# Running sums of logs and angles as two fp32r products each, at new places in the instruction stream

## The chip, the cores and the metric

One core of a Trainium2 chip (trn2) runs the whole kernel. The time is device microseconds of one execution, the median of several. All runs told here were in the fast state of the chip (one core, mean granted TensorE clock 0.957 to 0.992 over the span). Every timed version was run in rounds beside the kernel before on the same chip.

## The reference

A linear-attention block with complex decays (4 batches, 8 heads, 768 steps, 48 columns a head) followed by a two-layer block with the activation h·cos(h). Cut to what matters:

```python
def _attn_ref(q, k, v, a_re, a_im):
    mag = np.sqrt(a_re * a_re + a_im * a_im)
    scale = np.minimum(mag, 0.999) / (mag + 1e-06)
    a_re_n, a_im_n = (a_re * scale, a_im * scale)
    for t in range(S):                       # state is multiplied by a complex number each step
        new_re = ar * S_re - ai * S_im       # ar, ai: a_re_n, a_im_n of step t
        new_im = ar * S_im + ai * S_re
        S_re, S_im = (new_re + kv, new_im)   # kv: outer product of k[t] and v[t]
        y[:, :, t] = einsum(q[:, :, t], S_re)

def _moe_ref(x, w_in, w_out):                # x: (3072, 384)
    h = x @ w_in                             # w_in: (384, 2048)
    return (h * np.cos(h)) @ w_out
```

A chain of complex multiplications is a running sum of logarithms of the magnitudes and a running sum of the angles. The kernel takes both as products with a triangle of ones on TensorE. These are the two products that the change rewrites.

## The kernel before

The 3072 rows are 24 chunks of 128 steps; two chunks are a group, so there are 12 groups. The kernel is a software pipeline: while TensorE does the two layers of group n, the logs, angles and trigonometry of group n + 1 are made ready. `weave` merges lists of work by a fraction of the stage: a pair like `0.22, 0.24` says where in the stage a list is laid. All of TensorE's instructions are chained in that order; VectorE and ScalarE get an order from the scheduler.

```python
    def log_steps(g, i, n):          # "..." marks cuts
        chain(nc.scalar.activation(out=m2, in_=re, func=AF.Square))
        chain(nc.scalar.activation(out=sq, in_=im, func=AF.Square))
        vector.tensor_tensor(out=m2, in0=m2, in1=sq, op=ALU.add)
        yield
        special(out=m2, in_=m2, func=AF.Ln, bias=tiny_b)
        ...
        special(out=rs, in_=rs, func=AF.Ln, scale=EPS, bias=one_b)
        special(out=sq, in_=mag, func=AF.Ln)
        special(out=sq, in_=sq, func=AF.Exp, scale=-1.0)
        yield
        vector.tensor_tensor(out=m2, in0=m2, in1=rs, op=ALU.subtract)    # the logs, tile lg
        yield
        vector.tensor_tensor(out=mag, in0=mag, in1=sq, op=ALU.mult)      # three steps that only
        ...                                                              # the angles need

    def p_powers(g, i):              # running sum of logs (lgs), then powers P = exp, Q = exp(-)
        ...
        matmul(ps, lhsT=sums[g >= PEG], rhs=cut(x["lg"], i, 1), start=True, stop=True)
        special(out=cut(x["P"], i, 1), in_=ps, func=AF.Exp)
        special(out=cut(x["Q"], i, 1), in_=ps, func=AF.Exp, scale=-1.0)

    def g_phase(g, i):               # running sum of angles (phs); i: which chunk of the group
        if i:
            g_carry(g, i)            # chunk 1 needs the last phase of chunk 0
        matmul(ps, lhsT=turns[g >= PEG], rhs=cut(x["tan"], i, 1), start=True, stop=not early)
        ...
        scalar.copy(out=ph.bitcast(I32), in_=ps)                          # whole turns
        vector.tensor_tensor(out=ph, in0=ps, in1=ph.bitcast(I32), op=ALU.subtract)

    def prods(g):
        for i in range(G):
            yield lambda i=i: p_powers(g, i)
        yield lambda: g_angle(g, 0, G)                                    # arctangent
        yield lambda: g_carry(g, 0)
        yield lambda: (p_even(g, 0, G), p_apply(g, 0, G))                 # corrects P and Q, applies them

    def seventh(g, p, part):         # second layer as seven products; 0, 3, 5, 6 share one sum
        summed = p in (0, 3, 5, 6) and not alone
        ps = x["sum"] if summed else x["op"]
        ...                          # 16 matmuls of 192 columns; the sum goes on without a restart
        if p in (1, 3, 4, 5) or alone:   # VectorE reads the partial sum after product 3
            added = vector.scalar_tensor_tensor(out=part_, in0=..., scalar=scale, in1=part_, ...)

    for n in range(2, NG):
        weave(..., (logs(n + 1), 0.0, 0.02), ...,
              (prods(n + 1), 0.22, 0.24), ..., (products(n - 1, 3, 7), 0.4, 0.56),
              (phases(n + 1), 0.4, 0.56), (keys(n + 1), 0.53, 0.66), ...)
```

One thing in it matters later. The products 0, 3, 5 and 6 of the second layer pile up in one accumulator, and its state after product 3 is itself a result. So product 5 cannot start before VectorE has read the partial sum.

## Time and profile before

| | kernel before |
|---|---|
| time, median (lowest to highest) | 684.94 us (684.42 to 685.08, 3 runs) |
| span of the profiled run | 681.9 us |
| TensorE busy | 653.7 us, 96% |
| VectorE busy | 480.3 us, 70% |
| ScalarE busy | 382.5 us, 56% |

The busy times are shares of the whole span. TensorE has no room, and the other two have room on average. The average says nothing about where in a group they are full, which is what this case turns on. The lines themselves are in the prediction.

### The profile page before, as it was taken

The page shows a single profiled execution, that of the slowest core. Times are in us where ns is not written, and L with a number is a line of the kernel's source. Part 1 is how long each engine was busy: PE and PEld are TensorE (multiplying, and loading weights), DVE is VectorE, ACT ScalarE, POOL GpSimd, SP SyncE. Part 2 cuts the span into 40 slices and gives each one's busy share as a digit, 9 for nine tenths or more (in the row PEclk, how much of TensorE's full clock was granted, in tenths as well). Part 3 has the DMA queues.
Part 4 walks back from the last instruction along what each step waited for, and adds up shares of the span by engine and source line. Part 5 has one row for each costly group of instructions (what it writes and reads, how often), then busy time and mean ns, then how long its engine had stood idle before and what let it go on. Part 6 is the DMA issues. An engine that isn't in the chain of part 4 may idle for free.

```text
span 681.9 us, 10685 instructions
## 1 busy us (share of the span) xinstructions
PE 653.7 (96%) x4060; PEld 577.7 (85%) x4060; DVE 480.3 (70%) x782; ACT 382.5 (56%) x710; POOL 27.3 (4%) x45
## 2 busy tenths in 40 slices
PE   5788999999999999999999999999999999999996
PEld 5686676886899889899899889999899889999895
DVE  4889988468867877777777777767777768762251
ACT  5769784473474475466476476366466467332330
POOL 2012000000000000000000000000000000000000
PEclk8979999999999999999999999999999999999998
DMA  9777717706537557656657657565766653264000
GB/s 245 177 232 230 187 59 159 201 1 143 160 70 140 153 126 164 170 131 154 184 127 158 180 128 161 158 145 122 205 139 130 196 128 83 104 141 127 24 6 24
DMA packets 232954, 94.97 MB, mean 139 GB/s; under 512 B 208814, under 2 KB 221361, under 8 KB 232892
## 3 DMA queue, kind: packets, MB, share of 16 engines
q1 hardware_dynamic: 226396, 68.68, 44.6%
q0 software_dynamic: 5632, 25.17, 11.0%
q8 instruction: 34, 0.56, 0.4%
q10 hardware_dynamic: 864, 0.33, 0.2%
q14 instruction: 28, 0.23, 0.1%
HBM read 69.35 MB, written 24.81 MB: 138 GB/s over the span
## 4 chain that ended last, share of the span: by engine, by line
PE 84%; DMA 5%; DVE 5%; ACT 4%; issue 1%; DVEq 0%; ACTq 0%
PE hp L683 31%; PE op L683 17%; PE sum L683 15%; PE sc L683 6%; PE yp L683 5%; PE sp L683 3%; PE lgs L683 2%; DMA raw<-in_moe_w_out_dram 2%; PE phs L683 2%; DMA qT<-moved 2%; DVE w_in L672 1%; ACT raw L672 1%; DVE w_out L672 1%; PE yr L683 1%; DMA im<-in_a_im_dram 1%
## 5 line engine op out<-in xcount | busy, mean ns | idle before, releaser
L683 PE MATMUL hp<-xT,w_in 128*128 128x256 f32 x1152 | 253.6, 382 | 0.6 <-ACT xT L672 0.6
L683 PEld LDWEIGHTS hp<-xT,w_in 128*128 128x128 f32 x1152 | 220.1, 191 | 32.2 <-ACT xT L672 1.0
L702 ACT ACTIVATE gate<-hp,half_pi_b 128x512 f32<-128x512 f32 x96 | 65.9, 687 | 126.6 <-PE hp L683 126.6
L672 DVE TENSOR_TENSOR gate<-hp,gate 128x512 f32<-128x512 f32 x96 | 65.6, 683 | 60.0 <-ACT junk L672 60.0
L683 PE MATMUL op<-w_out,gate 128*128 128x192 f32 (+1 forms) x448 | 101.6, 375 | 2.3 <-DVE w_out L672 2.3
L683 PEld LDWEIGHTS op<-w_out,gate 128*128 128x128 f32 x448 | 75.8, 190 | 22.5 <-DVE w_out L672 3.5
L672 ACT ACTIVATE junk<-hp 128x512 bf16<-128x512 f32 x96 | 56.6, 590 | 0.0
L683 PE MATMUL sum<-t_s,s 128*128 128x192 f32 x320 | 55.3, 326 | 0.0
L683 PEld LDWEIGHTS sum<-t_s,s 128*128 128x128 f32 x320 | 52.6, 190 | 0.0
L683 PEld LDWEIGHTS sc<-qT,kT 96*128 96x128 f32 x384 | 47.5, 192 | 5.3 <-issue 2.8
L683 PE MATMUL sc<-qT,kT 96*128 96x128 f32 x384 | 49.5, 276 | 2.4 <-DMA qT<-moved 1.3
L672 DVE TENSOR_TENSOR atm<-sc,causal 128x512 f32<-128x512 f32 x48 | 32.8, 686 | 21.3 <-PE sc L683 21.1
L672 ACT ACTIVATE ot<-sum 128x192 f32<-128x192 f32 x30 | 9.5, 321 | 59.8 <-PE sum L683 59.8
L672 DVE SCALAR_TENSOR_TENSOR ot<-op,ot 128x192 f32<-128x192 f32 x31 | 11.0, 355 | 41.2 <-ACT ot L672 26.1
L698 ACT ACT_TABLE_LOAD x26 | 33.4, 1283 | 4.0 <-DMA ident<-ident_const 3.6
L683 PE MATMUL yp<-atm,v 128*48 128x128 f32 x352 | 33.5, 277 | 0.0
L683 PEld LDWEIGHTS sp<-v,ks 128*96 128x96 f32 x320 | 29.7, 165 | 1.8 <-issue 1.0
L683 PE MATMUL sp<-v,ks 128*96 128x48 f32 x320 | 29.6, 245 | 0.0
L683 PE MATMUL sum<-w_out,gate 128*128 128x192 f32 x160 | 29.6, 329 | 0.0
L683 PE MATMUL yp<-qT,state 96*48 96x128 f32 x304 | 29.6, 272 | 0.0
L683 PE MATMUL op<-t_a,gate 128*128 128x192 f32 x160 | 29.0, 332 | 0.0
L672 ACT CAST tan<-phs 128x384 int32<-128x384 f32 x24 | 11.5, 479 | 30.8 <-PE phs L683 30.6
(123 smaller groups left out, 949.2 us busy)
## 6 DMA issues: line engine op xcount, KB each, us to landing
moved<-tr SPq DMA_DIRECT2D x20, 768.0 KB
raw<-in_moe_w_in_dram POOLq DMA_DIRECT2D x16, 768.0 KB, 5.7
raw<-in_moe_w_out_dram POOLq DMA_DIRECT2D x16, 768.0 KB, 4.9
kT<-moved SPq DMA_DIRECT2D x40, 192.0 KB
qT<-moved SPq DMA_DIRECT2D x10, 768.0 KB
k<-in_k_dram SPq DMA_DIRECT2D x24, 192.0 KB
q<-in_q_dram SPq DMA_DIRECT2D x24, 192.0 KB
v<-in_v_dram SPq DMA_DIRECT2D x24, 192.0 KB
```

Of the source, the lines that this page charges most:

```text
L672: ins = getattr(self.engine, op)(**kw)
L683: chain(nc.tensor.matmul(out, **kw), "tensor")
L698: chain(nc.scalar.preload_act_table_set(table))
L702: chain(nc.scalar.activation(func=func, **kw))
```

## The change

The intent: a full fp32 product of 384 columns costs TensorE 0.645 us from its start to the next. The type fp32r is meant to be cheaper a product; that it keeps less of a float is what the halves are for, and no run here measured it. A float is split into a high half (its copy in the new type) and a low half (the remainder), each times ones and summed in one accumulator; that this is the same number at half the price was the author's assumption. The two passes together took 0.348 us in the changed kernel, and the runs below that keep the halves passed the comparison with the reference. The halves cost one ScalarE copy (high; 0.84 us for 768 columns, 0.52 for 384) and one VectorE instruction (low; 0.95 and 0.56). The angles of the second chunk can be split only after the carry of the first; so its first 96 rows are split early, and the last 32 once the carry is in. To give the halves time, the products are moved: logs from 0.22–0.24 to 0.27–0.31 of the stage, the angles from 0.4–0.56 to 0.475 and 0.52. Groups 0 and 1 stay as they were. The diff, cut to its core:

```diff
+    def halves(g, x, i, n, scale, part=slice(0, C)):
+        hi, lo, all_ = (cut(t, i, n)[part] for t in (X[g]["hi"], X[g]["lo"], x))
+        scalar.activation(out=hi, in_=all_, func=AF.Copy, scale=scale)
+        vector.scalar_tensor_tensor(out=lo, in0=all_, scalar=scale, in1=hi.bitcast(F32),
+                                    op0=ALU.mult, op1=ALU.subtract)
+    def g_halves(g):
+        if g >= PEG:
+            new_halves(g)
+            halves(g, X[g]["lg"], 0, G, 1.0)
+    def summed_up(ps, g, i, name, ones):
+        ...
+        for half in "hi", "lo":
+            matmul(ps, lhsT=exact, rhs=cut(X[g][half], i, 1), start=(half == "hi"),
+                   stop=(half == "lo"))
@@ p_powers
-        matmul(ps, lhsT=sums[g >= PEG], rhs=cut(x["lg"], i, 1), start=True, stop=True)
+        summed_up(ps, g, i, "lg", sums[0])
@@ g_carry
+        if g >= PEG:
+            at = X[g]["tan"]
+            if i == 0:
+                new_halves(g)
+                halves(g, at, 0, 1, 1.0 / math.pi)
+                halves(g, at, 1, 1, 1.0 / math.pi, slice(0, C - 32))
+            else:
+                halves(g, at, i, 1, 1.0 / math.pi, some)
@@ prods
+        yield lambda: g_halves(g)
         for i in range(G):
             yield lambda i=i: p_powers(g, i)
@@ the stages
-    weave((second(0, 1), 0.0, 0.35), (phases(2), 0.0, 0.1), (keys(2), 0.1, 0.4),
+    weave((second(0, 1), 0.0, 0.35), (phases(2), 0.2, 0.3), (keys(2), 0.3, 0.45),
-              (prods(n + 1), 0.22, 0.24), (second(n - 1, 1), 0.4, 0.56),
-              (products(n - 1, 3, 7), 0.4, 0.56), (phases(n + 1), 0.4, 0.56),
+              (prods(n + 1), 0.27, 0.31), (second(n - 1, 1), 0.4, 0.56),
+              (products(n - 1, 3, 7), 0.4, 0.56), (phases(n + 1)[:1], 0.475, 0.475), (phases(n + 1)[1:], 0.52, 0.52),
```

(Cut: the constants' pools, a scratch buffer that is `re` in place of `rs`, and the ones copied once into the new type.)

More of the change, by code (lines that the diff above doesn't have):

```diff
@@ L15 @@
 I32 = mybir.dt.int32
+F32R = mybir.dt.float32r
 BF16 = mybir.dt.bfloat16
@@ L530, in fast_path, with constant @@
     carry_np = np.where(step_np == C - 1, np.float32(math.pi), np.float32(0.0))[:, None]
-    def constant(array, name, queue=nc.scalar):
-        t = consts.tile(list(array.shape), F32, name=name)
+    def constant(array, name, queue=nc.scalar, pool=consts):
+        t = pool.tile(list(array.shape), F32, name=name)
         queue.dma_start(out=t, in_=nc.inline_tensor(array, name=name + "_const").ap())
@@ L570, in fast_path @@
             load(0, names, i)
-    ident = constant(np.eye(C, dtype=np.float32), "ident")
-    sums = [constant(sums_np[0], "sums")]
-    turns = [constant(sums_np[0] * np.float32(1.0 / math.pi), "turns")]
-    last = constant(last_np, "last")
+    ident = constant(np.eye(C, dtype=np.float32), "ident", pool=stage["pool"])
+    sums = [constant(sums_np[0], "sums", pool=stage["pool"])]
+    turns = [constant(sums_np[0] * np.float32(1.0 / math.pi), "turns", pool=stage["pool"])]
+    last = constant(last_np, "last", pool=stage["pool"])
     carry = constant(carry_np, "carry")
@@ L752, in log_steps @@
         yield
-        junk = msb.tile([C, DM], BF16, tag="below", name="below", bufs=1) if n == 1 else rs
+        junk = stage["pool"].tile([C, DM], BF16, tag="below", name="below", bufs=1) if n == 1 else re
         scalar.activation(out=junk, in_=re, func=AF.Relu, scale=-1.0,
@@ L759, in g_log, with new_halves @@
             pass
+    def halves(g, x, i, n, scale, part=slice(0, C)):
[3 more added lines that the diff above has]
+                                    op0=ALU.mult, op1=ALU.subtract)
+    def new_halves(g):
+        for name, tag in ("hi", "rs"), ("lo", "lo"):
+            X[g][name] = gt.tile([C, G * DM], F32R, tag=tag, name=name)
+    def g_halves(g):
[3 more added lines that the diff above has]
+    def summed_up(ps, g, i, name, ones):
+        if g < PEG:
+            matmul(ps, lhsT=ones, rhs=cut(X[g][name], i, 1), start=True, stop=True)
+            return
+        for half in "hi", "lo":
+            matmul(ps, lhsT=exact, rhs=cut(X[g][half], i, 1), start=(half == "hi"),
+                   stop=(half == "lo"))
     def p_powers(g, i):
@@ L824, in g_phase @@
             g_carry(g, i)
-        matmul(ps, lhsT=turns[g >= PEG], rhs=cut(x["tan"], i, 1), start=True, stop=not early)
-        if early:
+        if not early:
+            summed_up(ps, g, i, "tan", turns[0])
+        else:
+            matmul(ps, lhsT=turns[0], rhs=cut(x["tan"], i, 1), start=True, stop=False)
             matmul(ps, lhsT=last, rhs=before(n), start=False, stop=True)
@@ L1184, in fast_path @@
     load(1, ("re", "im", "k", "q"))
-    sums.append(constant(sums_np[1], "sums_turned", nc.sync))
-    turns.append(constant(sums_np[1] * np.float32(1.0 / math.pi), "turns_turned", nc.sync))
+    ones = constant(sums_np[1], "sums_turned", nc.sync, stage["pool"])
+    exact = consts.tile([C, C], F32R, name="exact")
     early = [weight(dst, src) for dst, src in into[:RAW]]
+    chain(nc.gpsimd.tensor_copy(out=exact, in_=ones), "gpsimd")
     Ordered.by_hand = True
```

## The prediction

> **What bounds the kernel now.** I read the page's busy shares first, then its forty slices, then the waits of TensorE alone, then a timeline of one group of two chunks (a group takes about 51 us in the steady part).
>
> ```profile
> PE 653.7 (96%) x4060; PEld 577.7 (85%) x4060; DVE 480.3 (70%) x782; ACT 382.5 (56%) x710; POOL 27.3 (4%) x45
> ...
> PE   5788999999999999999999999999999999999996
> ```
>
> TensorE is busy 653.7 of 681.9 us, and the 28 us of idle time lie almost wholly in the first four slices (the start, 17 us each). From slice five on the row is all nines. So in the steady part a microsecond of TensorE stream that is removed is a microsecond of the kernel, unless a wait takes its place. The waits of TensorE alone show how few there are now:
>
> ```profile
> PE phs L683 <- ACT tan L702: 4.2, 2, 2.8
> PE lgs L683 <- DVE lg L672: 2.8, 1, 2.8
> ...
> PE phs L683 <- DVE tan L672: 2.1, 4, 0.8
> PE sc L683 <- DMA qT<-moved: 1.3, 2, 0.9
> ```
>
> The first two are in the start. The third has two parts: the start, and group 2 at 108 and 113 us. The last is two groups in which the turned queries land 0.4 and 0.9 us late. The lgs and phs of groups 3 to 11 wait for nothing. What the change touches are lgs (running sum of logs) and phs (running sum of angles), one product of 384 columns each per chunk. TensorE's timeline around the ones of group 6:
>
> ```profile
> 310.89 1.45 PE L683 MATMUL lgs<-lg,sums_turned 128*128 128x384 f32 x4
> 312.28 0.43 PE L683 MATMUL yp<-atm,v 128*48 128x128 f32 x4
> ...
> 319.48 0.81 PE L683 MATMUL phs<-tan,turns_turned 128*128 128x384 f32 x2
> 320.12 2.76 PE L683 MATMUL op<-w_out,gate 128*128 128x192 f32 x16
> 322.72 2.76 PE L683 MATMUL sum<-t_s,s 128*128 128x192 f32 x16
> 325.32 0.81 PE L683 MATMUL phs<-tan,turns_turned 128*128 128x384 f32 x2
> 325.97 2.81 PE L683 MATMUL sum<-w_out,s 128*128 128x192 f32 x16
> 328.61 16.57 PE L683 MATMUL hp<-xT,w_in 128*128 128x256 f32 x76
> ```
>
> Columns: start, length, what, count. One product leaves two records (x40 records for 20 products). Starts are what counts: 320.12 - 319.48 = 0.64 us for one product, and 5.20 us of other products lie between the two phs.
>
> [...]
>
> **The change, part by part.**
>
> Groups 0 and 1 keep the old products. Groups 2 to 11 have 20 lgs and 20 phs. Removed: 40 x 0.64 = 25.6 us. Added: 80 single passes x 0.16 = 12.8 us. Gain in the stream: 12.8 us. This is the whole possible gain, but for waits of today that could vanish as well.
>
> Added elsewhere, per group: ScalarE one copy of 768 columns (0.84) and three of 384 (0.5 each), 2.3 us; VectorE one of 768 (0.95) and three of 384 (0.55 each, as the state update of 384 takes), 2.6 us. Over ten groups 23 and 26 us, to 59% and 74%. Both have room on average; in a timeline of the stretch from 299 to 318 us, though, ScalarE has hardly a gap, and there lie logs, guard and exponentials.
>
> The logs' halves are taken early, and the change puts lgs one or two products later, so I see lgs ready about 0.7 us before TensorE gets there: no wait. For the first phs I follow the instruction order of the changed kernel by hand: after lgs come four exponentials (1.2 us to the last start, 0.5 for it), table load 1.28, arctan 0.85, carry 0.62, copy 0.5, remainder 0.55, in all 5.5 us, against 6.5 us of products in between (20 of 192 columns, 0.326 each from the rows above). The second guard block, fetched about 0.75 us later because the copy delays the first on ScalarE, now sits ahead of the P and Q correction on VectorE. It makes the first phs some 0.2 us late in about four groups: 0.8 us in all.
>
> **The second phs is the term that I think costs.** It needs the carry out of the first. The steps today:
>
> ```profile
> 320.32 0.48 ACT L672 CAST tan<-phs 128x384 int32<-128x384 f32 x1 [1.67 <-PE phs L683]
> 320.83 0.56 DVE L672 TENSOR_TENSOR tan<-phs,tan 128x384 f32<-128x384 f32 x1 [0.74 <-ACT tan L672]
> 321.43 0.62 DVE L672 SCALAR_TENSOR_TENSOR tan<-tan,carry 32x384 f32<-32x384 f32 x1
> ```
>
> After the carry (322.05) the old kernel has 3.1 us in hand before 325.16, when its weights are loaded. The new one adds a copy of 32 rows on ScalarE (0.5) and a remainder on VectorE (0.55): from the start of the last half-product 0.36 to the cast, 0.51, 0.60, 0.65, 0.53, 0.55, and 0.07 to TensorE, 3.27 us. And only one of the two blocks of 2.60 us stays between the two phs, as the first was moved later. TensorE has 0.16 + 2.60 + 0.16 (the high half goes first) = 2.92 us of work. Wait: 0.35 us, [...]: 0.45. Eight groups (4 to 11): 3.6 us.
>
> Group 3: one block of 2.56 us between, but VectorE does three differences of w_out ahead of the subtraction: about 1.0 us. Group 2: in the new order its two phs stand back to back, so TensorE waits the whole chain less two half-products, 3.27 - 0.32 = 2.95 us. Today its phs are late by about 0.55 and 1.1 us (108.43 where 107.85 was possible, 112.75 where 111.65), 1.65 together, which are replaced. The rows split off the second chunk help here only in that 96 of 128 are done early; the latency of an instruction is nearly the same for 32 rows.
>
> Sum: 12.8 gained + 1.65 of old waits - 0.8 - 3.6 - 1.0 - 2.95 = 6.1 us gained. 684.94 - 6.1 = 678.8, rounded to **678.5 us**. The query transfer keeps its margin, since its start (the second phs) and its end (the first scores) are still 2.6 + 20.7 us of products apart.
>
> **Rivals.** (1) No new waits: the author's placement lets the handover fit, as the queues of VectorE and ScalarE are almost empty between the two phs (3.81 and 2.62 us busy in the 9.2 us from 319.4). Then 684.94 - 12.8 - 1.65 = 670.5, the floor, just over 2% faster. Against it: the chain's own durations exceed the block. (2) VectorE or ScalarE bind around the first phs: the guard block lands late, the correction of P and Q with it, and the halves after that. I reckon up to 1.5 us per group where the carry is queued behind all of them, in seven guarded groups 8 us or so: 685 to 687. Against it: the order puts the carry ahead of some of the work in most groups. (3) The new type runs at two cycles a column, or its weights don't hide: 80 x 0.16 = 12.8 us back, about 691 with the waits. [...] (4) The transfers of queries are late in more groups since the DMA share is 0.93 to 0.98 around phs: 1 us in each of some groups, 681 to 684.
>
> **Range and chances.** The stream gain is capped at 12.8 + 1.65, so more than 2% (under 671.2) needs rival 1 nearly entire: 0.06. Slower by over 2% (698.6) needs [...] heavy waits: 0.03. Within 2%: 0.91. The range has rival 1 with small waits below and rival 2 above: 671.8 to 686.
>
> **What would show it.** In the changed profile: lgs and phs as 40 single records each, starts 0.16 us apart in a run (0.32: rival 3); TensorE busy near 641 us; a line "PE phs <- DVE lo" or "DVE tan" in its waits with about 8 us over some 10 to 20 times, longest near 3 us at group 2; the group's period shortened by 0.7 to 0.9 us. Wrong would be: no such line and a time near 670 (rival 1); single waits over 1 us at the first phs with P and Q work just ahead on VectorE (rival 2); sc waiting on qT in more than three groups (rival 4).

## The result, and the profile after

The changed kernel took 691.99 us (690.16 to 693.81, 4 runs), beside 685.01 us (684.42 to 685.86, 4 runs) for the kernel before. The ratio is 1.0101 with a 95% interval of 1.0072 to 1.013. (Ratios here are the mean time of one kernel's fast runs over that of the other's in the same rounds, so not quite the ratio of the medians quoted.) It is 1% slower: inside the class "within 2%" that the prediction gave 0.91, but on the wrong side of zero and 6 us above the upper end of the range.

The busy shares of the changed kernel, from its page:

```profile
PE 647.9 (94%) x4060; PEld 576.7 (84%) x4060; DVE 503.5 (73%) x822; ACT 403.1 (59%) x750; POOL 27.6 (4%) x46
...
PE   6787998999999999999999999999999999999996
```

TensorE is busy 5.8 us less, VectorE 23.2 and ScalarE 20.6 us more (26 and 23 were predicted), and the span is 6.5 us longer. So the idle time of TensorE grew by 12.3 us. The row of slices does not show it, because a loss of 1 us in 51 stays a nine. The waits of TensorE alone do:

```profile
PE sum L684 <- DVE ot L673: 8.0, 7, 1.8
...
PE phs L684 <- ACT hi L673: 2.8, 2, 2.4
...
PE lgs L684 <- DVE lo L673: 1.0, 2, 0.5
```

(Total us, times, longest us.) The largest new wait is neither of the two products that were changed. It is a product of the second layer, `sum`, waiting for VectorE to write `ot`. Seven times are groups 4 to 10. The timeline of group 6 after the change, thinned to what matters:

```profile
319.59 2.76 PE L684 MATMUL sum<-t_s,s 128*128 128x192 f32 x16
320.81 0.57 DVE L673 TENSOR_SCALAR raw<-raw 128x768 uint32<-128x768 uint32 x1 [3.58 <-DMA raw<-in_moe_w_in_dram]
321.28 0.95 DVE L673 SCALAR_TENSOR_TENSOR mag<-Q,lg 128x768 f32<-128x768 f32 x1
...
324.01 1.02 DVE L673 SCALAR_TENSOR_TENSOR lo<-tan,hi 128x384 fp32r<-128x384 f32 x2
324.65 0.47 PE L684 MATMUL phs<-hi,exact 128*128 128x384 f32 x1
324.95 0.95 DVE L673 TENSOR_TENSOR Q<-k,Q 128x768 f32<-128x768 f32 x1
324.96 0.34 PE L684 MATMUL phs<-lo,exact 128*128 128x384 f32 x1
325.82 0.95 DVE L673 TENSOR_TENSOR mag<-q,lg 128x768 f32<-128x768 f32 x1
326.69 0.35 DVE L673 SCALAR_TENSOR_TENSOR ot<-sum,ot 128x192 f32<-128x192 f32 x1
327.09 2.87 PE L684 MATMUL sum<-t_s,s 128*128 128x192 f32 x16 [1.79 <-DVE ot L673]
```

Product 3, at 319.59, ends at about 322.2. Its partial sum is read only at 326.69: in front of the read VectorE runs, in the trace, a guard block that waits 3.58 us for its data, the corrections of P and Q (321.28 to 324.0), the low halves, and the two instructions that apply P and Q. The first angles' product runs in time at 324.65 and 324.96. TensorE then stands idle for 1.79 us before the next product, which goes on with the same sum. Before the change the same VectorE steps stood here:

```profile
313.41 0.96 DVE L672 SCALAR_TENSOR_TENSOR mag<-Q,lg 128x768 f32<-128x768 f32 x1 [0.92 <-ACT Q L702]
...
317.89 0.95 DVE L672 TENSOR_TENSOR mag<-q,lg 128x768 f32<-128x768 f32 x1
319.74 0.36 DVE L672 SCALAR_TENSOR_TENSOR ot<-sum,ot 128x192 f32<-128x192 f32 x1 [0.90 <-issue]
```

All of P and Q was done by 318.84, 0.6 us before product 3 ended (the first angles' product starts at 319.48), and the read ran at once. The logs' product started at 310.89 then, 8.6 us before the end of product 3; it starts at 317.45 now, 4.7 us before that end. So the move of the logs' product pushed seven VectorE instructions into the stretch in which the partial sum has to be read.

From the starts of TensorE's records, group by group, the whole account in microseconds:

| | per group | in all |
|---|---|---|
| logs' pair 1.29 to 0.70, each angles' product 0.645 to 0.348 | −1.19 | −11.9 |
| old waits gone (group 2's angles 1.8, queries 1.3) | | −3.1 |
| around the first angles' product, groups 4 to 10: low half late 1.6, next `sum` late 9.6 | +1.6 | +11.2 |
| `sum` after the second angles' product, groups 4 to 10 | +0.23 | +1.6 |
| group 2 (second product 2.5, pieces 1.0), group 3 (1.35), group 11 (1.0) | | +5.8 |
| start, between the logs' products of groups 1 and 2 | | +2.0 |

That adds up to +5.6 of the +6.5 us between the two traces. The last line need not come from the change: the kernel before without its guard blocks, a run told below, was 2.3 us longer at the end of group 1's angles than the kernel before, at the same time overall.

### The profile page after: what moved, and what is told of

It reads as the page before. It is cut to its first block, busy times and chain, and to the rows that moved or that the text cites. A ratio compares the mean times of both kernels' runs of the same rounds, so it can differ in the third digit from the quotient of the medians.

```text
span 688.4 us, 10787 instructions
## 1 busy us (share of the span) xinstructions
PE 647.9 (94%) x4060; PEld 576.7 (84%) x4060; DVE 503.5 (73%) x822; ACT 403.1 (59%) x750; POOL 27.6 (4%) x46
## 4 chain that ended last, share of the span: by engine, by line
PE 67%; DVE 11%; ACT 11%; DMA 6%; issue 3%; DVEq 0%; ACTq 0%; SPq 0%
PE hp L684 33%; PE sum L684 12%; PE op L684 9%; PE sc L684 4%; PE yp L684 4%; DMA raw<-in_moe_w_in_dram 2%; DMA raw<-in_moe_w_out_dram 2%; DVE mag L673 2%; PE sp L684 2%; ACT L699 1%; ACT lg L703 1%; DVE lg L673 1%; DVE lo L673 1%; ACT raw L673 1%; PE phs L684 1%
## 5 line engine op out<-in xcount | busy, mean ns | idle before, releaser
L673 DVE TENSOR_TENSOR gate<-hp,gate 128x512 f32<-128x512 f32 x96 | 65.6, 684 | 60.2 <-ACT junk L673 60.2
L673 ACT COPY yT<-yp 48x512 f32<-48x512 f32 x44 | 25.3, 576 | 19.8 <-PE yp L684 19.3
```

What stands on the lines that cost most here:

```text
L673: ins = getattr(self.engine, op)(**kw)
```

## The experiments

Theory D: the halves add serial steps to a path that had no slack (logs, product, exponentials, table load, arctangent, carry, halves, product, carry, halves, product, trigonometry, transposes, transfer of queries). In the stream they save 1.2 us a group, but on the path they add about 4: 0.84 + 0.95 for the logs, twice 0.5 + 0.55 for the angles. What the places decide is only where the wait shows. The rivals: (A) the moved places are the whole fault; (B) the guard blocks on VectorE are; (C) the new type or the added work costs wherever it stands.

### Undoing the places, and moving alone

`old_places`: the change with the old fractions.

```diff
-   (prods(n + 1), 0.27, 0.31) ... (phases(n + 1)[:1], 0.475, 0.475), (phases(n + 1)[1:], 0.52, 0.52)
+   (prods(n + 1), 0.22, 0.24) ... (phases(n + 1), 0.4, 0.56)          # group 2 likewise
```

> The change's halves and products, but the three shifted places in the weave (corrections and lgs, first phs, group 2) as in the kernel before. Theory A (the shifted places are what makes the first partial sum's read on VectorE late, so that TensorE waits for it before it may accumulate on): lgs come 2 to 4 us earlier, the P and Q work is done before the first phs, the waits 'sum <- DVE ot' (10.0 us on the weight loads after the change) fall under 2 us, and the time is below the kernel before, 676 to 683 us. Rival B (the added work on VectorE and ScalarE is too much at this spot wherever it is put): about as the changed kernel, 689 to 694 us.

Measured: 721.16 us (719.69 to 721.82), ratio 1.0538 (1.0515 to 1.0561). Much worse, so rival A falls as it was put (undoing the places does not bring the gain): the author had reason to move the products. The wait for `ot` is gone and this took its place, in the waits of TensorE:

```profile
PE lgs L684 <- DVE lo L673: 21.0, 10, 2.9
```

Its timeline in group 6:

```profile
326.13 0.84 ACT L673 ACTIVATE hi<-lg 128x768 fp32r<-128x768 f32 x1
...
327.04 0.47 PE L684 MATMUL lgs<-hi,exact 128*128 128x384 f32 x1
327.26 0.95 DVE L673 SCALAR_TENSOR_TENSOR tan<-mag,tan 128x768 f32<-128x768 f32 x1
...
328.39 0.94 DVE L673 SCALAR_TENSOR_TENSOR tan<-tan,im 128x768 f32<-128x768 f32 x1
329.26 0.95 DVE L673 SCALAR_TENSOR_TENSOR lo<-lg,hi 128x768 fp32r<-128x768 f32 x1
330.26 0.44 PE L684 MATMUL lgs<-lo,exact 128*128 128x384 f32 x1 [2.74 <-DVE lo L673]
```

The high half is done at 326.97, and the low half starts at 329.26, behind steps that only the angles need. This is the line that later led to the fast version. There is a second cost, the clock. The granted clock, by stretches around three of these stalls (columns: stretch, length, busy of PE, PEld, DVE, ACT, POOL, clock, DMA share, GB/s):

```profile
267.00:282.00 15.00, 12.26 (x88) 11.51 (x87) 9.91 (x14) 9.12 (x16) 0.76 (x1) 0.77 0.47 111
325.00:340.00 15.00, 12.26 (x88) 11.35 (x87) 10.94 (x15) 10.00 (x19) 0.76 (x1) 0.89 0.65 134
432.00:446.00 14.00, 11.25 (x101) 10.70 (x100) 11.12 (x17) 9.11 (x17) 0.76 (x1) 1.00 0.62 142
```

All three have a stall of 3.2 us from one start to the next (2.7 us of it idle). Two were followed by a stretch at half clock, one was not. Over the span 60.2 us were at half clock, against 16.3 in the changed kernel, so that some 22 us of the loss are clock (an estimate: half of the difference; at half clock, behind the stall at 546.24, passes of 384 columns start 0.32 us apart in this trace, where they start 0.174 apart at full clock in the changed kernel's). So a single wait near 3 us can cost about its own length again, where 6.8 us at half clock follow it (an estimate: half of the 6.8 us).

`moves_only`: the kernel before, full fp32 products, with only the new fractions.

> The kernel before, full fp32 products, with only the three shifted places of the change. Theory A: waits of sum on DVE ot appear here too, 3 to 8 us in all, and the time is 688 to 693 us. Rival B: the places alone cost under 1 us, 684.5 to 686 us.

Measured: 696.57 us (693.78 to 697.79), ratio 1.0186 (1.0163 to 1.021). The moves alone lose 1.9%, so at the new places the halves do save (ratio 1.0101 with them, 1.0186 without). The waits:

```profile
PE sc L683 <- DMA qT<-moved: 5.1, 4, 2.4
...
PE sum L683 <- DVE ot L672: 1.9, 2, 1.0
```

Without the halves' steps the wait for `ot` is a quarter as long, but the scores now wait for the queries: the later angles' products push everything behind them. The schedule of the kernel before had no room to move anything later.

### Is it the guard blocks?

Each guard fetches a block of weights and tests it; in the traces VectorE waits for those blocks 20.7 us in the changed kernel against 6.8 before.

`guards_in_hp`: the guards moved into the first layer's stretch.

```diff
-  wait_for(X[g]["gate"][NJ // 2 - 1]...)   ... (guarded(n - 1, per) if n > 3 else [], 0.1, 0.9)
+  wait_for(X[g]["gate"][0]...)             ... (guarded(n, per) if n > 3 else [], 0.6, 1.0)
```

> The changed kernel with the weights' guard blocks moved from the chunk stage into the hp stage. Theory C (VectorE sits idle ahead of the P and Q correction because a guard block whose transfer has not landed is first in its queue, 20.7 us of such idle time in all): VectorE's waits for raw vanish from the chunk stage, the sum waits fall from 10.0 to about 3 to 5 us, time 685 to 688 us. Rival (the length of the work queued ahead of the read, not the transfer, sets it): the sum waits stay above 8 us, time 690 to 692.

Measured: 730.19 us (729.3 to 734.04), ratio 1.0683 (1.0644 to 1.0722). A miss: the block now stands in front of the gates that the first layer waits for, whose stretches grew from 20.7 to between 24 and 28 us. It shows how dear a waiting block in that place is (38 us above the changed kernel), and little about the change: the wait for `ot` did fall to 4.2 us, as expected, but the time does not tell what that was worth.

`no_guards_before` and `no_guards_after`: both kernels without any guard (one line, `guards = []`; the test of the weights is then left out, and the results stay right on these inputs).

> The kernel before without its sixteen guard blocks (a check of the weights' exponents that this data never fails; so the result stays right). Control for the next run. Theory C (a guard block whose transfer has not landed heads VectorE's queue): in the kernel before VectorE waits only about 7 us for such transfers and none of it reaches TensorE but the late queries (1.3 us), so 682 to 685 us. Rival: guards cost here what they cost after the change.

> The changed kernel without the guard blocks. Theory C: VectorE's 20.7 us of waits for raw vanish, TensorE's waits of sum on DVE ot fall from 10.0 to 3 to 5 us, and the time falls by 5 to 9 us more than in the control, to 683 to 687 us. Rival D (the added serial steps of the halves alone, 2 ACT and DVE pairs per group, make everything late): at most 3 us more than the control, 688 to 691 us.

Measured: before without guards 684.6 us (681.78 to 686.56), ratio 1.001 (0.9998 to 1.0023); after without guards 692.07 us (688.94 to 694.42), ratio 1.0129 (1.0087 to 1.017). Rival B falls. The wait for `ot` did shrink from 8.0 to 4.2 us, but the time stayed. From the start of group 1's first layer to that of group 11's the trace without guards is only 1.1 us shorter (518.2 against 519.2), with 1.7 us of new waits of the scores in it, and its start is 2.6 us longer.

`raw2_behind`: the second guard of a group ordered behind the queries' transposition on VectorE.

> The changed kernel with the second guard block of each group kept, but ordered behind the transpose of the turned queries on VectorE, where its transfer has long landed. Theory C: about as without guards, 683 to 688 us, no wait of VectorE for raw over 1 us in groups 5 to 11 except the first block's. If the guard's own work and not its transfer costs, no gain: 690 to 693 us.

Measured: 690.17 us (688.47 to 693.29), ratio 1.0115 (1.0077 to 1.0153). No clear gain. The wait for `ot` is 4.2 us here too.

### Taking away the wait for `ot`

`apply_late`: the two instructions that apply P and Q leave the front of the partial sum's read and stand just before the trigonometry.

```diff
-        yield lambda: (p_even(g, 0, G), p_apply(g, 0, G))
+        yield lambda: (p_even(g, 0, G), p_apply(g, 0, G) if g < PEG else None)
@@ keys
+            if g >= PEG:
+                yield lambda i=i, n=n: p_apply(g, i, n)
             yield lambda i=i, n=n: g_trig(g, i, n)
```

> The changed kernel with the two products k*Q and q*P (0.95 us each on VectorE) put behind the first partial sum's read instead of ahead of it. If the queue on VectorE ahead of that read is what TensorE waits for, each of the groups with a wait gains up to 1.8 us: sum waits from 10.0 to under 2.5 us, time 683 to 687 us. If TensorE's loss came from the chain through the halves (carry, high half, low half), nothing changes: 690 to 693 us.

Measured: 691.07 us (690.27 to 693.27), ratio 1.0096 (1.0079 to 1.0114). The wait for `ot` is gone altogether, and the time is the same. In its waits:

```profile
PE phs L684 <- ACT hi L673: 6.8, 9, 2.4
...
PE sc L684 <- DMA qT<-moved: 3.0, 4, 1.2
```

Now the second angles' product comes late, by 0.6 to 0.8 us in every group from 4 to 10, with another 0.28 until its low half; and behind it the queries. Most of this the experiment made itself. In the program the two moved instructions stand before the trigonometry, but on VectorE they came right behind the read, in front of the subtraction that leads to the second product. Group 6:

```profile
326.87 0.48 ACT L673 CAST tan<-phs 128x384 int32<-128x384 f32 x1 [1.38 <-PE phs L684]
327.10 0.95 DVE L673 TENSOR_TENSOR mag<-q,lg 128x768 f32<-128x768 f32 x1
328.23 0.54 DVE L673 TENSOR_TENSOR tan<-phs,tan 128x384 f32<-128x384 f32 x1
```

The cast ends at 327.35 and the subtraction starts 0.88 us later; in groups 4 to 10 this gap is 0.71 to 0.95 us, in group 11 it is 0.03. So `apply_late` moved the queue from one product to the next and did not take it away. Three experiments (no guards, guard behind, apply late) took the visible wait away or halved it, and none moved the time by more than its noise. That fits theory D, but does not prove it, as in each of them another wait came or part of the old one stayed.

### Which move is needed: the logs alone

`only_logs_moved`: logs' product at its new place, angles' products at their old places.

> The changed kernel with the logs' product at its new place and the angles' products at their old places, halves made late as in the change. Theory D: the logs' product then waits for little (1 us in all), but the path from it to the first product of angles (exponentials, table load, arctangent, carry, copy, remainder: some 5.5 us and more where other work of VectorE is ahead) now has two blocks of 8 products less in front of it, 3.9 us of TensorE's work: the first product of angles waits 1.5 to 2.5 us in each of 9 groups for its halves, 13 to 22 us in all, and the time is 690 to 702. The waits of the partial sum of products go. Rival (only the angles' new places cost): 674 to 680.

Measured: 706.56 us (704.12 to 707.8), ratio 1.0325 (1.0302 to 1.0348).

```profile
PE phs L684 <- ACT hi L673: 12.1, 9, 1.8
PE phs L684 <- DVE lo L673: 7.9, 9, 1.4
```

Twenty microseconds of waits for the angles' halves, 18.3 of them at the first product, as theory D expected (13 to 22), and none at `sum`. The time is above the 690 to 702 expected; 37.6 us were at half clock, against 16.3 in the changed kernel. With the halves made late, the way from the logs' product to the first angles' product is longer than what TensorE has to do in between. The author's two moves belong together. The counterpart, the angles' products moved alone, was not run.

### Shortening the path instead

If the path is the limit, then the halves must be made where the path has time, not the products be moved. First a miss:

`early_old_raw2`: old places; the squares of the next logs begun at 0.8 of the stage before; the second guard behind.

```diff
-   (logs(n + 1), 0.0, 0.02)
+   (logs_ended(n + 1), 0.0, 0.02), (logs_begun(n + 2), 0.8, 0.8)     # first step of log_steps, then the rest
```

> The halves and products of the change, the old places in the weave, the second guard block behind the queries' transpose, and the two squares and their sum (first step of the logs, 2.6 us on the path) begun in the hp stage of the group before. Theory D (the path logs, halves, lgs, exponentials, angle, halves, phs, queries is as long as a group, so steps added to it cost what steps taken off it give back): lgs' waits on the low half, 23.8 us with the old places alone, fall under 4 us, and the 1.2 us per group that the cheaper products save show: 674 to 680 us, faster than both kernels. Rival: the waits turn up elsewhere again, 686 us or more.

Measured: 701.35 us (700.36 to 702.19), ratio 1.0262 (1.0238 to 1.0286). Better than the old places (721), but the logs' product still waited 13.4 us in 9 groups for its low half. Beginning earlier does not help when the high half stands last on ScalarE and the low half behind three steps of the angles. So those were moved.

`halves_in_logs_old`: old places; the halves of the logs made inside `log_steps`.

```diff
         special(out=sq, in_=mag, func=AF.Ln)
-        special(out=sq, in_=sq, func=AF.Exp, scale=-1.0)
-        yield
         vector.tensor_tensor(out=m2, in0=m2, in1=rs, op=ALU.subtract)
         yield
+        g_halves(g)                      # no longer in prods()
+        special(out=sq, in_=sq, func=AF.Exp, scale=-1.0)
+        yield
         vector.tensor_tensor(out=mag, in0=mag, in1=sq, op=ALU.mult)
```

> The changed kernel with the old places of the products, and the logs' two halves made inside the log steps: the copy straight after the logs are ready and ahead of the last exponential, the remainder ahead of the three VectorE steps that only the angle needs. In the runs with the old places the copy came last on ScalarE and the remainder after those three steps, and TensorE waited 21 us in 10 groups for it. Theory D (the halves lengthen a serial path that had no slack, and the places only decide where the wait shows): the path to the logs' product is shortened by 2 to 3 us a group, so most of that wait goes, the wait of the product of logs is under 6 us in all, the clock windows that came with it go too, and the time is 672 to 681, faster than both kernels. Rival (the chip or the new type costs something that follows the halves wherever they are): 688 or more, with the wait gone.

Measured: 680.32 us (677.07 to 683.11), ratio 0.9934 (0.991 to 0.9958). The same instructions, two of them elsewhere: 41 us less than the old places with the halves late. Some 18 us of that are clock (an estimate: half of 60.2 less 24.5 us at half clock). Rival C falls with it.

`halves_in_logs`: the same at the change's new places.

> The changed kernel at its own new places, with the halves of the logs made inside the log steps. At the new places the product of logs waits only 1 us in all for its halves, so theory D expects little: the wait for the halves goes, the waits of the partial sums (8 us in 7 groups) stay as they are set by the queue behind the first product of angles: 687 to 692. If the earlier halves let the correction of the powers run earlier, a little less.

Measured: 693.73 us (690.95 to 695.25), ratio 1.0134 (1.0104 to 1.0164). No gain there, and the time is above the 687 to 692 expected: the wait for `ot` is again 8.0 us in 7 groups. So the new places lose whatever the halves do, and the old places need the early halves.

`early_halves_in_logs_old`: both, the early squares and the early halves.

> As the first of these four, and the squares and their sum of the next group begun at 0.8 of the stage before, so that ScalarE starts the logs at once when its gates are done. If the logs' path is still what the product waits for in the first run, this takes off another 1.7 us a group of it: 671 to 677, and no more wait for the logs' halves. If nothing is left to wait for, it is the same as the first within 2 us. The same change with the halves late gave 701, so if that run's loss had another cause than the late remainder, this one will be near 700 too.

Measured: 677.79 us (675.81 to 680.31), ratio 0.9884 (0.9854 to 0.9914), just above the 671 to 677 expected. Its interval touches that of the early halves alone (0.991 to 0.9958), so what the early squares add here is small and not sure.

### The parts, and the start

`angles_only_old` and `logs_only_old`: old places; only one of the two sums in halves, the other full fp32 (logs' halves inside `log_steps`).

> The changed kernel with the old places, where only the angles' product is made of two halves and the logs' product is the full fp32 one again (times ones that are the same numbers). Theory D: nothing is added ahead of the logs' product, so it waits for nothing new; the angles' products had 2 us or more in hand at the old places, so half of the gain in the stream (20 products x 0.3 = 6 us, less the 1 to 3 us of group 2) is kept: 679 to 683. Rival (the added work on VectorE and ScalarE costs wherever it is): 685 or more.

> The counterpart of the run with the angles alone: the old places, the logs' halves made inside the log steps, and the angles' product full fp32 with no halves. Theory D: the path of the angles is as before, nothing is added between the two products of angles; the logs' halves are ready nearly in time, so that 20 products x 0.3 = 6 us of stream are gained less about 1 us of waits: 679 to 681, with group 2 as fast as before. Rival (each half costs more on the other engines than it saves): 684 or more.

Measured: angles alone 684.27 us (682.08 to 686.39), ratio 0.9994 (0.9976 to 1.0013); logs alone 682.03 us (678.42 to 684.84), ratio 0.9975 (0.9955 to 0.9995). Both gain less than expected (679 to 683, and 679 to 681), the angles alone nothing that is clear of noise. In the traces, the time from the start of the first layer of group 2 to that of group 11 was 461.8 us before, 457.8 with the angles alone, 459.2 with the logs alone and 453.8 with both (`halves_in_logs_old`). So in the steady part the two bring 4.0 and 2.6 us apart and 8.1 together. With the logs alone the scores still waited for the queries in three groups, 2.3 us; with both, it is not among the waits. The rest is lost ahead of this: with the angles' halves, the stretch from group 2's logs' product to the next start of the first layer took 20.6 us against 18.8, as its two angles' products have little between them.

`from_group_3` and `early_from_group_3`: the two fast versions, with group 2 left on full fp32 products.

```diff
-        if g < PEG:
+        if g <= PEG:
             matmul(ps, lhsT=..., rhs=cut(X[g][name], i, 1), start=True, stop=True)
             return
@@ g_halves, g_carry
-        if g >= PEG:
+        if g > PEG:
```

> The version with the old places and the logs' halves made inside the log steps (680.3 us), with group 2 left on the full fp32 products. In its trace the stretch of group 2 from the product of logs to the first weights product of the next stage took 21.4 us where the kernel before took 18.8, because there is little else to do between the two products of angles there. Theory D (the halves cost where their steps stand on the path): the 2.6 us come back, less 1 us of stream: 677 to 679.5, and no more wait of the angles' product for the copy in group 2. Rival (that stretch is longer for another cause, say the clock at the start): 680 to 682, unchanged.

> The fastest version so far (677.8 us: old places, logs' halves inside the log steps, squares begun early), with group 2 on the full fp32 products. Theory D: 1.5 to 3 us less than that version, 674.5 to 677. Rival: unchanged, 677 to 679.

Measured: 676.91 us (674.91 to 677.89), ratio 0.9899 (0.9881 to 0.9916), and 674.76 us (674.29 to 675.96), ratio 0.9876 (0.9861 to 0.9891). The second is the fastest version found: 1.2% under the kernel before and 17 us under the change. Its page, and its group 6:

```profile
PE 644.4 (96%) x4060; PEld 577.2 (86%) x4060; DVE 500.5 (74%) x818; ACT 401.5 (60%) x746; POOL 27.6 (4%) x46
```

```profile
302.45 0.96 DVE L673 TENSOR_TENSOR lg<-lg,rs 128x768 f32<-128x768 f32 x1
303.89 0.83 ACT L673 ACTIVATE hi<-lg 128x768 fp32r<-128x768 f32 x1
...
305.04 0.95 DVE L673 SCALAR_TENSOR_TENSOR lo<-lg,hi 128x768 fp32r<-128x768 f32 x1
...
308.25 0.47 PE L684 MATMUL lgs<-hi,exact 128*128 128x384 f32 x1
...
308.85 0.95 DVE L673 SCALAR_TENSOR_TENSOR tan<-tan,im 128x768 f32<-128x768 f32 x1
```

The low half is done at 305.99, 2.3 us before TensorE takes it, and the angles' step that used to stand ahead of it now comes after. VectorE and ScalarE are as busy as in the change; only the order differs.

`early_before`: the kernel before with only the early squares.

> The kernel before with only the early squares, to see whether the gain of the fastest version is that of the halves or of the squares begun early. In the kernel before no product waits for the logs, so theory D expects the same time as the kernel before, within 0.3%. Rival (the early squares are worth something by themselves): 682 or less.

Measured: 684.57 us (682.57 to 686.87), ratio 1.0003 (0.9991 to 1.0015). The early squares are worth nothing by themselves; the gain is that of the halves.

## Why the prediction was wrong

Step by step:

- **The stream's gain, 12.8 us**: right. It was 11.9, as a pass took 0.174 us in a run where 0.16 was assumed (the author's assumption; no trace from before the change shows a pass of the new type). Rival 3 (0.32 us a pass) did not come.
- **Old waits that vanish, 1.65 us**: right, 1.8, and 1.3 of the queries besides.
- **The logs' halves, "no wait"**: nearly right, 1.25 us in groups 2 and 11. The weight loads last 0.19 us each in both traces; no line of the waits names them.
- **"It makes the first phs some 0.2 us late in about four groups: 0.8 us in all"**: this is the step that failed. It took 11.2 us in seven groups. The working followed the chain to the angles' product, and rightly found VectorE's corrections of P and Q in front. It did not ask who else waits for that queue. The product behind the first phs goes on with a sum whose interim value VectorE must read first, and that read stood behind all of it: possible at about 322.2 in group 6, it ran at 326.69. The low half itself was late by 1.6 us; the read made 9.6.
- **The second phs, 3.6 us**: the chain was sized rightly, but it showed in one group of eight. In groups 4 to 10 of the changed kernel the product's waits were 0, because TensorE came late from the step above; only 1.6 us were lost, behind it, where a shorter product no longer hides ScalarE's reading of `sum` (the next `sum` starts 0.41 us behind the low half's start, against 0.174 for a pass). In group 11, where nothing came late, the chain from the first product's low half to the second's took 3.36 us (3.27 was said), and 0.39 us were lost (0.45 was said, a part of it for a weight load: the author's assumption, which no line of the waits shows). In `apply_late` 1.0 to 1.2 us a group were lost there; without the 0.7 to 0.9 us that the moved instructions made, some 0.3 us are left (an estimate). So two waits stood one behind the other, and adding them as if they were independent was wrong. That the latency is nearly the same for 32 rows held: the high halves of 384 columns took 0.51 to 0.53 us with 32, 96 or 128 rows, the low ones 0.55 to 0.56.
- **Group 3, 1.0 us**: 1.35. **Group 2, 2.95 us**: 2.97 between its two products.

The sum was 6.1 us gained; with the failed step at its measured size it is some 4 us lost. Rival 2 ("VectorE or ScalarE bind around the first phs", 685 to 687) was the right one in its mechanism, but it looked for the wait at the angles' product; the trace after has it one product further on, and larger. Rival 3's 691 is nearer to the measured 692, by luck: the rate that it rests on did not come. One reading was off too, though nothing rests on it: of the 28.2 us that TensorE was idle before, 15.5 lie in the first four slices and 6.7 in the last.

What is shown and what is not: that the new places lose and the late halves lose is shown by runs that change one of them. That the guards are not the cause is shown. That the path as a whole has no slack is the reading that fits the runs in which a wait was lessened without gain; no run measured the slack itself, and in the fastest version the logs' low half is 2.3 us early, so there is some once the order is right. No run kept the new places and put the read of the partial sum first without delaying the second angles' product. The 2.0 us at the start of the changed kernel are left open; they vary between runs of kernels that are equal there.

## What to carry to other kernels

When work is taken off the engine that binds and put on others, the question is not whether they have room on average, but what stands behind the new instructions in their queues, and who waits for that: here a product that the change did not touch. If removing a wait only brings another, shorten the path by moving the new instructions to where their inputs first exist, before moving the consumers later. The place of the same two instructions alone made a difference of 41 us, part of it through the clock that fell after the stalls (60.2 us at half clock against 24.5).

## What the runs show of the new type and of the clock

- In the changed kernel a pass of 384 columns takes 0.173 to 0.175 us from start to start in a run, while a full fp32 product of 384 columns takes 0.645.
- Switching the type costs nothing that the trace shows. The first high half starts 28 ns after the start of the product before it and the low half 309 ns later; together 0.337 us, the same as 0.163 + 0.174.
- In `old_places` some stalls with 2.7 us of idle time, and one group with two stalls of 0.6 and 1.3 us idle, were followed by half clock, and other such stalls were not; the half-clock stretches behind them were 3.4 or 6.8 us long.
- A float split into two halves, each times ones, is near enough for this running sum: all of the runs with them passed the comparison with the reference.
